# First chunk of a state-space scan: B and C loaded by rows of four tokens and turned once for all batches

## Chip, cores and metric

One NeuronCore of a Trainium2 chip runs the whole kernel. The metric is device time in microseconds, from the first to the last instruction with what lies around them; the median of the runs is quoted.

## What is computed

Inputs: `x` [4 batches, 8 heads, 768 tokens, 32], decays `a` [4, 8, 768], `B` and `C` [4, 8, 768, 16], three weight matrices (256 x 1536 twice, 1536 x 256), all float32. First a scan with decay, in chunks, then a gated feed-forward layer on its 3072 x 256 result:

```python
cum = np.cumsum(np.log(a_chunk), axis=-1)
L = np.exp(cum[..., :, None] - cum[..., None, :]) * causal
M = np.einsum('bhin,bhjn->bhij', Cc, Bc) * L
y = M @ xc + (Cc @ state) * np.exp(cum)[..., None]
state = decay_full * state + sum_j(Bc_j xc_j * decay_from_j)
...
gate = 1 / (1 + np.exp(-(y @ w_gate)))
out = (gate * (y @ w_val)) @ w_out
```

## The kernel before

The 768 tokens are taken in six chunks of 128 (two halves of 64 each). Chunk 0 is worked batch by batch by the class `FirstUnit`, one unit for each of the four batches; later chunks by the class `Scan`, all batches together. Of a unit: `spread` has TensorE multiply `apart` (the clipped decays of all batches, one head's in each column block) by `of_unit`, which copies a batch's decays to all partitions (tile `pa`), and VectorE runs a multiplying scan over it (tile `ab`). `products` turns the batch's B and C (tile `pt`), ScalarE copies them out (`bct`), TensorE forms the products C B (`pcb`). `before` and `decays` make C and B with decays (`cd`, `bd`). `result` weighs `pcb` with the scan (`m`), multiplies by `x` (`py`, `mm`), VectorE keeps the right blocks (`sm`, `mr`), TensorE adds the part of the first half's state, and ScalarE takes the result out (`xw`, in `take`). `state` makes the state that chunk 1 starts from. `first_products` makes the running products of the decays (`pp`).

The feed-forward layer then runs over column tiles f = 0 to 11 of each chunk of 512 rows. For chunk 0, f = 0 is worked in halves (`halves_of`, tile `pgv`), f = 1 to 5 with plain float32 weights (`gate` and `value`, tiles `pg` and `pv`), and from f = 6 on in the format fp32r with high and low parts of the weights (`part_w`, tile `w`) and of x (`parts_of_x`, tiles `xh` and `xl`). `split_w` rounds the weights (tile `wr`): two VectorE steps, two of ScalarE, one of GpSimd. Float32 matmuls of 512 columns leave two records in the trace, fp32r ones a single record.

All loads of the head are issued on SyncE's queue: the decays, then B and C of a batch with two DMAs each (`load_bc`: 128 partitions, for each of 8 heads one piece of 16 numbers, 64 bytes), then x (pieces of 128 bytes) and the weights (pieces of 2 KB). Three PSUM buffers (`ps_mm`) go round among `pa`, `pt`, `pp`, `mm` and the feed-forward products; `ps_y` holds one `py`.

The order of everything is made when the program is built: `run` takes generators of steps, each with an engine, a planned cost and needs, and gives each engine the ready step with the lowest place in the table `DUES`, among those that can start soonest. A letter behind a place (d, p, a) fixes the engine where a step can go to two. `keep_warm` adds matmuls on an identity where the plan has TensorE idle; `WARM` lists the matmuls on zeros at the very start (widths in blocks of 128 columns).

Of the kernel before, what the change touches and what calls it, by code (L numbers as in the profile page):

```python
# [8 lines left out]
F32 = mybir.dt.float32  # L9
# [9 lines left out]
    "": "0 1", "b0": "2", "w0": "3", "b3": "4", "b1": "5", "products0": "6 7 9 13 18", "products0_0": "8 11 28",  # L19
    "spread3": "10 15", "split0": "12 16 19 24 32", "b2": "14", "spread1": "17 23", "spread0": "20 29", "x0": "21",  # L20
    "before0_0": "22p 27", "decays0_3": "25", "x1": "26", "products0_1": "30 34 42", "w1": "31", "spread2": "33 41",
    "x3": "35", "result0_0": "36 46 50 56 63 69", "decays0_0": "37p", "products0_3": "38 44 51", "x2": "39",
    "decays0_1": "40", "w2": "43", "before0_1": "45 47d", "products0_2": "48 55 64", "decays0_2": "49",
    "result0_1": "52 60 66 70 77 82", "early0_0": "53", "before0_3": "54p 57", "w3": "58",
    "result0_3": "59 78 87 91 95 98", "bq1_2": "61", "split1": "62 68 79 85 96", "r": "65", "before0_2": "67p 74p",
    "state0_0": "71", "w5": "72", "result0_2": "73 92 99 100 105 111", "early0_1": "75", "w4": "76",
    "xparts": "80 88d 116 209d", "bq1_0": "81", "half0_0": "83 103 112 117", "state0_1": "84", "w13": "86",
    "w6": "89", "early0_3": "90", "split2": "93 97 102 107 115", "bq1_3": "94", "early0_2": "101", "w7": "104",
    "state0_3": "106", "split3": "108d 119 124 126 139", "bq1_4": "109", "half0_1": "110 118 123 128",
    "state0_2": "113", "w9": "114", "w10": "120", "clip": "121 129 135", "gate0_1": "122 134",  # L30
# [12 lines left out]
    "split12": "241d 244 249 253 265", "value0_8": "247 254", "part10": "248 252", "gate0_9": "251 259",
    "split17": "255 262 274 278 282", "value0_9": "256 264", "part11": "257 260d", "split15": "258d 275 284 289 296",
    "gate0_10": "261 268", "split14": "263d 266 270 272 277", "value0_10": "267 276 280d 322", "w16": "269",
    "early1": "271", "gate0_11": "273 281", "value0_11": "279 291 295d 316d",
    "proj0_0": "283 304 337 345 347 350 376", "part17": "285 292", "bq2_4": "286", "decays1": "287 299 300 305 311d",
    "bq2_0": "288", "bq2_6": "290", "bn2": "293", "bq2_2": "294", "part0": "297 308d",
    "proj0_1": "298 325 352 361 364 430 460", "a2_0": "301", "cq2_4": "302", "bq2_5": "303", "bq2_3": "306",
    "cq2_5": "307", "cq2_1": "309", "cq2_6": "310", "part1": "312 336d", "a2_1": "313",  # L50
    "split16": "314 317 320 323 328", "cq2_2": "315", "scan1": "318 332 335 340", "before1": "319d", "bq2_7": "321",
    "cq2_0": "324", "weigh1": "326 329 333 338 344 353 355 357 359", "bq2_1": "327", "cq2_3": "330", "cq2_7": "331",
    "bn3": "334", "part2": "339 341", "state1": "342 349d", "part3": "343 346d", "part4": "348 351d",
    "part5": "354 356d", "part12": "358 360p", "gate1_0": "362 370", "p2_0": "363", "p2_1": "365",
    "value1_0": "366 374 378a 382", "part13": "367 371d", "p2_3": "368", "p2_2": "369", "x2_": "372",
    "gate1_1": "373 381", "part14": "375 377p", "value1_1": "379 387 397 406d", "turned2": "380 384",
# [81 lines left out]
PE0 = 5.6  # L138
# [1343 lines left out]
```

## Time and profile before

| what | value |
|---|---|
| median of 3 runs | 345.69 us (345.6 to 346.02) |
| the profiled execution | 345.54 us |
| its span, first to last instruction | 343.7 us, so 1.84 us lie around it |
| busy share of the span | TensorE 98%, VectorE 64%, GpSimd 52%, ScalarE 44% |

The span is read as a head, in which chunk 0 is scanned and TensorE has gaps, and a rest, in which it has next to none. A busy TensorE is not one at its peak: filler matmuls and cold ones count as busy.

### The profile page before, as it was taken

To read this page: it belongs to the slowest core of one execution; us is meant where nothing else is said; L and a number is where in the kernel's file an instruction comes from. 1 tells how busy PE (TensorE), PEld (TensorE's weight loads), DVE (VectorE), ACT (ScalarE), POOL (GpSimd) and SP (SyncE) were. 2 spreads that over 40 slices of the span, in tenths; PEclk is the share of its full clock that TensorE was granted. 3 is DMA by queue.
4 is the path that set the end of the run, shared out by engine and by line. 5 is a ranking of instruction groups with operands and counts; after the bars stand their busy time and mean duration, and the time that the engine had idled before them with its cause. 6 is when DMAs were issued, how large, how long until landed. Compare 5 with 4: busy or idle time off the path is not lost.

```text
span 343.7 us, 7948 instructions
## 1 busy us (share of the span) xinstructions
PE 337.9 (98%) x3144; PEld 261.7 (76%) x3144; DVE 220.2 (64%) x377; ACT 150.2 (44%) x277; POOL 180.0 (52%) x181
## 2 busy tenths in 40 slices
PE   8899999999999999999999999999999999999996
PEld 3474587457888888888888888888888888888885
DVE  5889978956879872456666954566064646856221
ACT  4476987124744230136411513361047557645300
POOL 4646265431646434566774545489427885355500
PEclk9999999999999999999999999999999999999999
DMA  6996899871674376476543621108123733220032
GB/s 107 180 352 209 256 272 146 162 132 35 94 159 62 90 109 159 97 139 89 145 100 102 85 76 21 63 3 297 72 36 91 240 89 110 110 61 2 0 58 67
DMA packets 100247, 40.16 MB, mean 117 GB/s; under 512 B 88754, under 2 KB 91826, under 8 KB 99570
## 3 DMA queue, kind: packets, MB, share of 16 engines
q1 hardware_dynamic: 97906, 39.39, 49.3%
q10 hardware_dynamic: 2304, 0.26, 0.5%
q8 instruction: 25, 0.41, 0.5%
q14 instruction: 12, 0.10, 0.1%
HBM read 30.00 MB, written 9.63 MB: 115 GB/s over the span
## 4 chain that ended last, share of the span: by engine, by line
PE 98%; DVE 1%; ACT 0%; issue 0%
PE pg L981 17%; PE pv L981 17%; PE ux L1121 6%; PE acc L1121 6%; PE po L1017 5%; PE po L1013 5%; PE po L1019 5%; PE po L1018 5%; PE acc L1224 5%; PE uz L1121 5%; PE pg L972 2%; PE pv L972 2%; PE po L1251 2%; PE pcb L706 2%; PE pcb L691 2%; PE pcb L647 2%
## 5 line engine op out<-in xcount | busy, mean ns | idle before, releaser
L981 PE MATMUL pg<-xh,w 128*128 128x512 f32 x168 | 59.0, 392 | 0.0
L981 PE MATMUL pv<-xh,w 128*128 128x512 f32 x168 | 58.9, 391 | 0.0
L927 POOL TENSOR_TENSOR h<-g,h 128x512 fp32r<-128x512 f32 x27 | 38.3, 1420 | 24.4 <-ACT h L925 17.2
L921 DVE TENSOR_TENSOR g<-pv,g 128x512 f32<-128x512 f32 x38 | 26.1, 688 | 30.1 <-PE pv L981 29.1
L903 ACT ACTIVATE g<-pg 128x512 f32<-128x512 f32 x47 | 28.0, 596 | 39.4 <-PE pg L981 37.2
L981 PEld LDWEIGHTS pg<-xh,w 128*128 128x128 f32 x168 | 31.5, 188 | 6.7
L981 PEld LDWEIGHTS pv<-xh,w 128*128 128x128 f32 x168 | 31.5, 188 | 6.6
L497 POOL TENSOR_TENSOR wr<-wr 128x512 int32<-128x512 int32 x18 | 20.5, 1143 | 26.8 <-ACT wr L495 13.0
L981 PE MATMUL pg<-xl,w 128*128 128x512 f32 x84 | 32.7, 389 | 0.0
L981 PE MATMUL pv<-xl,w 128*128 128x512 f32 x84 | 32.7, 389 | 0.0
L1017 PE MATMUL po<-h,w 128*128 128x512 f32 x76 | 30.8, 405 | 0.0
L1019 PE MATMUL po<-h,w 128*128 128x512 f32 x76 | 29.6, 390 | 0.0
L1018 PE MATMUL po<-h,w 128*128 128x512 f32 x76 | 29.6, 389 | 0.0
L577 DVE TENSOR_TENSOR_SCAN ab<-ab,delta 128x512 f32<-128x512 f32 x20 | 28.1, 1424 | 0.0
L925 ACT CAST h<-g 128x512 fp32r<-128x512 f32 x26 | 16.0, 619 | 24.2 <-DVE g L921 24.0
L1048 POOL TENSOR_TENSOR c<-c,c 128x512 f32<-128x512 f32 x13 | 17.2, 1326 | 17.9 <-ACT c L1176 9.2
L1048 POOL TENSOR_TENSOR h<-c,h 128x512 fp32r<-128x512 f32 x16 | 21.0, 1323 | 9.4 <-ACT h L1200 9.3
L1048 POOL TENSOR_TENSOR sw<-sw 128x128 f32<-128x128 f32 x36 | 18.9, 535 | 11.2 <-DVE sw L1048 10.2
L1028 DVE STREAM_TRANSPOSE o<-po 128x256 f32<-128x256 f32 x16 | 6.3, 430 | 21.2 <-PE po L1019 19.2
L1200 ACT CAST h<-c 128x512 fp32r<-128x512 f32 x24 | 14.9, 619 | 10.7 <-POOL c L1048 7.1
L981 PEld LDWEIGHTS pv<-xl,w 128*128 128x128 f32 x84 | 15.8, 188 | 3.2
L981 PEld LDWEIGHTS pg<-xl,w 128*128 128x128 f32 x84 | 15.8, 188 | 3.2
(197 smaller groups left out, 733.2 us busy)
## 6 DMA issues: line engine op xcount, KB each, us to landing
w_s<-sp SPq DMA_DIRECT2D x12, 512.0 KB
s<-w_s SPq DMA_DIRECT2D x12, 512.0 KB
ab<-a_z SPq DMA_DIRECT2D x10, 512.0 KB
wr<-in_moe_w_gate_dram SPq DMA_DIRECT2D x6, 512.0 KB
wr<-in_moe_w_val_dram SPq DMA_DIRECT2D x6, 512.0 KB
wr<-in_moe_w_out_dram SPq DMA_DIRECT2D x6, 512.0 KB
xn<-in_x_dram SPq DMA_DIRECT2D x5, 512.0 KB
out_dram<-o SPq DMA_DIRECT2D x144, 16.0 KB
```

Of the source, the lines that this page charges most:

```text
L497: nc.gpsimd.tensor_tensor(out=lw.bitcast(I32), in0=hw.bitcast(I32), in1=lw.bitcast(I32), op=ALU.add)
L577: nc.vector.tensor_tensor_scan(out=t, data0=t, data1=delta.rearrange("p h l -> p (h l)"), initial=0.0, op0=ALU.mult, op1=ALU.add,)
L903: nc.scalar.activation(gs[k, f], pm, AF.Sigmoid)
L921: nc.vector.tensor_tensor(out=g, in0=pm, in1=g, op=ALU.mult)
L927: engines[eng].tensor_tensor(out=hl, in0=g, in1=hh.bitcast(F32), op=ALU.subtract)
L981: nc.tensor.matmul(pm, w[:, part, kt, fs], xx[:, kt], start=(i == 0), stop=(i == 3 * NK - 1))
L1013: nc.tensor.matmul(acc, whole[NF + f // 2][:, f % 2, ms], hs[k, f], start=start, stop=stop)
L1017: nc.tensor.matmul(acc, hi, hh, start=start, stop=False)
L1018: nc.tensor.matmul(acc, hi, hl, start=False, stop=False)
L1019: nc.tensor.matmul(acc, lo, hh, start=False, stop=stop)
L1048: engines[eng].tensor_tensor(out=out, in0=in0, in1=in1, op=op)
L1121: nc.tensor.matmul(out, a[i], b[j], start=start and n == 0, stop=n == 2, skip_group_check=True)
```

## The change

B and C of chunk 0 are loaded like those of later chunks, in pieces of four tokens (256 bytes) for each head, onto 32 partitions a batch: four DMAs each, B's on SyncE's queue and C's on ScalarE's. One copy (`sorted_rows`) puts the four tokens of a row apart, four transposes turn all batches at once, and ScalarE writes B (`bt0`), C for both head groups (`cg0`) and C's second half (`ct0`) with the tokens in order; four more transposes of `bt0` give B by tokens (`bn0`). The decays are loaded twice, onto both halves of the partitions; the upper half keeps what rounding to fp32r leaves, so that `spread` is one fp32r product. `chosen_of` lets ScalarE do a step of VectorE's, some copies may go to GpSimd, two of the starting matmuls on zeros become the whole of `WARM`, and the table `DUES` is new throughout (in it `xparts` step 1 goes from VectorE to GpSimd, and the `state0` steps come later).

```diff
-WARM = (4, 4, 3)
-PE0 = 5.6
+WARM = (4, 4)
+PE0 = 4.7
-FIRST = "b0 x0 b1 x1 b2 x2 w0 b3 x3 w1 w2 w3 r w4 w5 w6 w7 w8 w9"
+FIRST = "bq0 w0 x0 x1 w1 x2 x3 w2 w3 r w4 w5 w6 w7 w8 w9"
...
-    of_unit = hp.tile([P, NB, P], F32, tag="h8", name="of_unit")
+    of_unit = hp.tile([P, NB, P], F32R, tag="h8", name="of_unit")
...
-        for tag, src in (("bn", b4), ("cq", c4)):
-            t = quad_of(tag, 0, H, N, bufs=2 if tag == "bn" else 1)
-            nc.sync.dma_start(t[:, b], src[:L, b * H : (b + 1) * H])
+    def load_first(tag, src, eng):
+        t = got[tag, 0] = ld.tile([P, H, NQ * N], F32, tag=tag, name=f"{tag}0", bufs=1)
+        rows = src[:, :, :L].rearrange("b h (t f) n -> b t h (f n)", f=NQ)
+        for b in range(NB):
+            eng.dma_start(t[32 * b : 32 * b + 32], rows[b])
...
+    def chosen_of(eng, out, local):
+        if eng == "dve":
+            return chosen(out.rearrange("p (o c) -> p o c", o=1), local.rearrange("p (o c) -> p o c", o=1), 1)
+        for g in range(NG):
+            gs = slice(g * D, (g + 1) * D)
+            nc.scalar.mul(out[:, gs], local[:, gs], of_g[:, g : g + 1])
...
-            yield step("pe", 0.45, [("bc", b)], [("tp", b)], banks=1)
-            nc.tensor.transpose(pt[:, :L], bn, eye)
-            nc.tensor.transpose(pt[:, L : 2 * L], cn, eye)
-            nc.scalar.copy(self.bct[:, 0], pt[:, :L])
-            for g in range(NG):
-                nc.scalar.mul(self.bct[:, 2 + g], pt[:, L : 2 * L], of_g[:, g : g + 1])
-            nc.scalar.copy(self.bct[:, 1, L2:], pt[:, L + L2 : 2 * L])
+            yield step("pe", 0.47, [("cg0",), ("bt", 0)], [("cb", 0, b)] + [("cb", 0)] * (b == NB - 1))
...
+            multiply(self.pcb, got["bt0"][:, b], got["cg0"][:, b])
...
+        copies[eng](t, got[tag, 0].rearrange("p h (f n) -> p f h n", f=NQ))
...
+        for f in range(NQ):
+            nc.tensor.transpose(pt[:, f * L : (f + 1) * L], got["sorted", tag][:, f].rearrange("p h n -> p (h n)"), eye)
...
+            nc.scalar.mul(got["cg0"][:, :, g].rearrange("p b (t f) -> p f b t", f=NQ), pt, of_g[:, g : g + 1])
+        nc.scalar.copy(got["ct0"].rearrange("p b (t f) -> p f b t", f=NQ), pt[:, :, :, L2 // NQ :])
+        engines[eng].tensor_tensor(out=got["ct0"], in0=got["ct0"], in1=got["p0"], op=ALU.mult)
+        nc.scalar.copy(got["bt0"].rearrange("p b (t f) -> p f b t", f=NQ), pt)
...
+        for b in range(NB):
+            nc.tensor.transpose(pt[:, b * L : (b + 1) * L], got["bt0"][:, b], eye)
+        nc.scalar.copy(t.rearrange("p b h n -> p (b h n)"), pt)
...
-    nc.gpsimd.memset(apart[R2:], 0.0)
-    nc.sync.dma_start(a0, av[:, :L].rearrange("k (o l) -> o k l", o=2))
+    for r, eng in enumerate((nc.sync, nc.scalar)):
+        eng.dma_start(a0[r * R2 : (r + 1) * R2], av[:, :L].rearrange("k (o l) -> o k l", o=2))
+    load_first("cq", Cm, nc.scalar)
     nc.scalar.activation(table, table, AF.Sigmoid)
...
+    nc.vector.tensor_copy(ah, ac)
+    nc.vector.tensor_tensor(out=ah[R2:], in0=ac[R2:], in1=ah[R2:].bitcast(F32), op=ALU.subtract)
```

## Rows read from the trace of the kernel before

**Rows 1.** The page, busy time and share of the span by engine.
```profile
PE 337.9 (98%) x3144; PEld 261.7 (76%) x3144; DVE 220.2 (64%) x377; ACT 150.2 (44%) x277; POOL 180.0 (52%) x181
```

**Rows 2.** Waits of TensorE, whole span: total us, times, longest.
```profile
PE py L706 <- ACT xw L834: 0.5, 1, 0.5
```

**Rows 3.** Timeline of TensorE: start us, us, engine line op out<-in xcount.
```profile
12.63 0.24 PE L706 MATMUL py<-m,xn 64*32 64x64 f32 x1
...
21.66 2.86 PE L962 MATMUL pgv<-xw,wr 128*128 128x256 f32 x12
...
41.53 0.83 PE L289 MATMUL pg<-eye 128*128 128x128 f32 x6
42.12 0.48 PE L981 MATMUL pg<-xh,w 128*128 128x512 f32 x1
```

**Rows 4.** Timeline of all engines, first 8 us.
```profile
0.74 1.28 ACT L1285 ACT_TABLE_LOAD   x1 [0.74 <-PEq L1465]
0.75 0.70 SPq L1283 DMA_DIRECT2D a<-in_a_dram  x1
...
3.24 0.23 DVE L1287 TENSOR_SCALAR ac<-a 64x64 f32<-64x64 f32 x1 [0.26 <-DMA a<-in_a_dram]
...
3.63 0.68 DVE L1289 TENSOR_TENSOR apart<-ac,head 64x512 f32<-64x512 f32 x1
...
3.82 0.34 PEld L237 LDWEIGHTS warm<-warm_sb 128*128 128x128 f32 x1 [0.52 <-issue]
...
4.67 0.34 PEld L237 LDWEIGHTS warm<-warm_sb 128*128 128x128 f32 x1 [0.52 <-issue]
...
6.19 1.02 PE L741 MATMUL pa<-apart,of_unit 128*128 128x512 f32 x2
...
7.25 1.22 DVE L744 TENSOR_TENSOR_SCAN ab<-pa,delta 128x512 f32<-128x512 f32 x1
```

**Rows 5.** Timeline of VectorE, ScalarE and GpSimd, chunk 0 and the start of f = 6.
```profile
11.38 0.69 DVE L695 TENSOR_TENSOR m<-pcb,ab 128x512 f32<-128x512 f32 x1
...
13.44 0.21 DVE L724 TENSOR_TENSOR sm<-py,mask 128x64 f32<-128x64 f32 x1
...
18.83 1.21 DVE L890 TENSOR_TENSOR xl<-xw,xh 128x512 fp32r<-128x512 f32 x1
...
20.73 0.23 DVE L724 TENSOR_TENSOR sm<-py,mask 128x64 f32<-128x64 f32 x1
...
41.19 0.68 DVE L890 TENSOR_TENSOR xl<-xw,xh 128x512 fp32r<-128x512 f32 x1
...
21.78 0.27 ACT L834 COPY xw<-mm 128x128 f32<-128x128 f32 x1 [0.53 <-PE mm L820]
...
18.46 1.04 POOL L497 TENSOR_TENSOR wr<-wr 128x512 int32<-128x512 int32 x1 [2.62 <-ACT wr L495]
```

**Rows 6.** Stretches: busy us (instructions) by engine, granted clock, DMA share, GB/s.
```profile
3.00:6.00 3.00, 3.00 (x6) 1.25 (x5) 1.25 (x4) 0.00 (x0) 2.01 (x5) 1.00 0.87 190
...
7.00:21.00 14.00, 12.48 (x306) 7.53 (x306) 12.33 (x24) 8.17 (x28) 6.93 (x13) 1.00 0.98 210
...
9.00:10.50 1.50, 1.50 (x21) 0.65 (x20) 1.50 (x2) 0.00 (x0) 1.50 (x3) 1.00 0.90 89
...
12.00:13.50 1.50, 1.28 (x66) 1.03 (x66) 1.50 (x4) 0.75 (x4) 0.63 (x3) 1.00 0.73 184
...
16.00:19.00 3.00, 2.46 (x76) 1.76 (x63) 2.33 (x10) 2.25 (x6) 0.54 (x1) 1.00 0.94 337
```

**Rows 7.** Groups by line and shape, 0 to 22 us: busy us, mean ns | idle before.
```profile
L695 DVE TENSOR_TENSOR m<-pcb,ab 128x512 f32<-128x512 f32 x4 | 2.7, 687 | 0.7 <-PE pcb L691 0.6
L765 ACT ACTIVATE bct<-pt,of_g 128x128 f32<-128x128 f32 x8 | 2.5, 374 | 0.0
...
L691 PE MATMUL pcb<-bct 32*64 32x128 f32 x64 | 1.9, 292 | 0.5 <-DVE m L695 0.5
...
L888 ACT CAST xh<-xw 128x512 fp32r<-128x512 f32 x1 | 0.6, 619 | 0.0
```

More of the change, by code (lines that the diff above doesn't have):

```diff
@@ L509, in part_w @@
             needs.append(("used", order[n - 2]) if order[n - 2] < NF else ("proj", 0))
-        yield step("act", ACT_SB, needs)
+        eng = yield step(("act", "pool"), (ACT_SB, 0.75), needs)
         hw, lw = halves.pop(i)
         hi, lo = parts_of(i)
-        nc.scalar.copy(hi, hw)
+        copies[eng](hi, hw)
         eng = yield step(("dve", "pool"), (DVE_SB, POOL_SB), [], [("w", i)], port=True)
@@ L791, in decays @@
             b = self.b
-            eng = yield step(("dve", "pool"), (0.28, 0.42), [("bc", b), ("scan", 0, b)], [("bdec", 0, b)], port=True)
+            eng = yield step(("dve", "pool"), (0.28, 0.42), [("bn0",), ("scan", 0, b)], [("bdec", 0, b)], port=True)
             if ("bd", 0) not in got:
@@ L825, in result @@
             self.take(1)
-            yield step("dve", 0.21, [], [("after", 0, b)], banks=-1)
+            eng = yield step(("dve", "act"), (0.21, 0.45), [], [("after", 0, b)], banks=-1)
             if ("mr", 0) not in got:
@@ L879, in tile_ssd_then_gated_ffn, with first_bn @@
+    def first_bn():
+        yield step("pe", 0.6, [("bt", 0)], banks=1)
+        pt = ps_mm.tile([P, 512], F32, tag="mm", name="pt_bn")
+        keep_warm(pt)
+        for b in range(NB):
+            nc.tensor.transpose(pt[:, b * L : (b + 1) * L], got["bt0"][:, b], eye)
+        yield step("act", ACT_MM, [], [("bn0",)], banks=-1)
+        t = quad_of("bn", 0, H, N, bufs=2)
+        nc.scalar.copy(t.rearrange("p b h n -> p (b h n)"), pt)
     hs, xb, xw, yw = {}, {}, [], {}
@@ L1062, in weight_sums @@
             sum_up(eng, out, in0, in1, op)
-        yield step("act", ACT_SB)
+        eng = yield step(("act", "pool"), (ACT_SB, 0.7))
         parts = hp.tile([P, 2, 512], F32R, tag="r1", name=f"sp{i}")
-        nc.scalar.copy(parts[:, 0], t[:, 1])
+        copies[eng](parts[:, 0], t[:, 1])
         eng = yield step(("dve", "pool"), (DVE_SB, POOL_SB), port=True)
@@ L1346, in initial @@
     def initial():
[L1348 removed]
+        made = [(k, c) for k in ("bt", "ct", "cd", "bdec") for c in (-1, 0) if c < 0 or k in ("cd", "bdec")]
         made += [("y", -1), ("first", 0, -1)]
```

87 lines of the change are left out of this document (53 added, 34 removed), and 233 rows, old and new, of the table DUES.

## The prediction

> **What bounds the kernel.** I read the page's busy shares first, then TensorE's waits, then its timeline, and only then the other engines, in the stretch where TensorE has gaps. TensorE is busy for 98% of the span [rows 1] and its longest wait on another engine after the start is 0.5 us [rows 2]. In the timeline the reader sees two parts. Up to 21.66 us its work comes in short pieces with gaps (the first unit's result begins at 12.63 us); from 21.66 on, feed-forward products of chunk 0 stand end to end [rows 3]. So the time is that of the moment at which TensorE gets into its unbroken part, plus work that this change leaves alone. A microsecond off the head is one off the total, as long as the engines that feed TensorE later come forward too; the place to watch is f = 6, where at 41.53 us fillers stand for 0.59 us before the first fp32r product at 42.12 [rows 3], which waits for the low part of x, begun by VectorE at 41.19 and 0.68 us long [rows 5].
>
> What sets the 21.66? Between 7 and 21 us VectorE is busy 12.33 of 14 us (88%), ScalarE 8.17 and GpSimd 6.93 [rows 6]. VectorE carries the four scans (1.22 us each [rows 4]), the four weighings (0.69 [rows 7]), the block picks, weight steps and an early `xl` of 1.21 us [rows 5]. Its last pick (`sm` of the last unit) is at 20.73 and the last take at 21.78 [rows 5]. VectorE's list sets the end of the head, and it starts only at 7.25, with the first scan [rows 4].
>
> **The change, step by step.**
>
> *Decays.* They land at about 3.24 us, `apart` is made from 3.63 to 4.31, the cold matmuls run to beyond 5.5 (weight loads at 3.82 and 4.67, 0.85 apart), the first spread runs at 6.19 for 1.02 us, and the scan begins at 7.25 [rows 4]. The change adds to VectorE a copy and a subtraction of 64 columns; the nearest row is the clip, 0.23 us [rows 4], so between 0.2 and 0.46 for both, and I take 0.4: `apart` is ready at 4.7. That it now spans 128 partitions costs nothing by rows: 64 partitions took 0.68 [rows 4], 128 took 0.69 [rows 7]. Two cold records of 384 columns go, each three quarters of 0.85 us, together 1.28, so the cold matmuls end by about 4.7 as well. The spread becomes one fp32r record of 512 columns, 0.48 us [rows 3], instead of 1.02. The first scan can start at 4.7 + 0.48 + 0.05, say 5.25: **2.0 us earlier**. Bounds: 1.4 (decays land 0.6 later, behind more DMAs) to 2.2. The memset of `apart` on GpSimd goes too, off the path.
>
> *B and C.* Eight DMAs of 64-byte pieces become eight of 256-byte ones, 8192 pieces become 2048, the bytes stay at 0.52 MB. While 64-byte pieces dominate, the DMA engines are 90% busy and move 89 GB/s; with x's 128-byte pieces 184; with mostly weights 337 [rows 6]. So B and C took some 5.8 us of the engines and now take between 2.85 (at 184) and 1.55 (at 337). On the queues: after the decays' issue, which ends at 1.45 [rows 4], four issues of at most 0.70 end at 4.25, and a landing follows an issue by 1.8 (1.45 to 3.24). That gives 6.0 us for B, bounds 5.2 and 7.0. ScalarE issues five DMAs itself, and its table load of 1.28 us now comes behind them: 4.25 + 1.28 = 5.5, before C is there. x and the weights, behind B on SyncE's queue, come forward by the 3 to 4 us of DMA time that is saved.
>
> *Turning.* Per batch two transposes and four ScalarE copies go (eight of these copies alone take 2.5 us [rows 7]). From B's landing to the first weighing there are now a copy of 512 columns (0.62, by the cast [rows 7]), four transposes (0.29 each at most, by the 128-column products; they overlap, so 0.7), a copy out (0.62), 16 products (1.9 / 4 = 0.48 [rows 7]) and four handovers of some 0.15: 3.0 us. So the first weighing starts at about 9.0, or 9.8 if the copies queue behind C's (0.62 each) and the three PSUM buffers; before it was at 11.38 [rows 5]. The first unit's result follows 1.25 us later as before (11.38 to 12.63), at 10.3 to 11.1. The turn back for `bn0` (0.7 + 0.62, and then `bd`) lies beside the weighing.
>
> *VectorE's list.* From its first scan to the last `sm` it took 20.73 - 7.25 = 13.5 us. `xl` moves to GpSimd (1.21), two state updates of some 0.2 (size of `sm`) move behind, one small step comes in: 13.5 - 1.3 = 12.2. From 5.25 that ends at **17.4, 3.3 us earlier**. By units: results at 10.8, 0.81 to the first `sm` (12.63 to 13.44), and three more units at a pace between 1.4 (0.81 + a take of 0.27 [rows 5] and handovers) and the old 2.43 ((20.73 - 13.44) / 3): 15.8 to 18.9, with 2.0 in the middle 17.6. Both agree; I take 3.3 for the head, bounds 1.8 to 4.9. The `xl` step beside GpSimd's own work at 18.46 took 1.21 instead of 0.68 [rows 5], so moving it to GpSimd may stretch a neighbour by up to 0.5; this is in the bounds.
>
> *f = 6 and the rest.* GpSimd and ScalarE get choices (copies of weight parts) and the table places the `split13` steps behind the last part of x, two VectorE steps fewer before it. The 0.59 us of fillers can go; I take 0.3, bounds 0 and 0.6. The rest of the new table I cost at nothing, since TensorE has no other wait there to lose; a new gap there is the cost if the cover is gone, bounded by the 0.5 of the largest present wait for each.
>
> **Sum.** 345.54 - 3.3 - 0.3 = 341.94 for a profiled execution; the median stands 0.15 above it: **342.1 us**. With all bounds of one side: 345.69 - 5.5 = 340.2 and 345.69 - 1.8 = 343.9.
>
> **Rivals.**
>
> *The head's gain is given back at f = 6.* TensorE reaches f = 1 earlier, but the weights need VectorE, ScalarE and GpSimd steps, and `xl` was the last by 0.25 us (41.87 against 42.12). If these come forward only by the 2.0 us of the first scan, minus 0.5 of stretched neighbours, the total gains 1.5: 344.2. For it: VectorE's 88% before. Against it: `xl`'s first part and `split13` are taken off.
>
> *TensorE stays cold.* The cold records stand 0.85 us apart, the spread's two records of the same columns took 1.02 together [rows 4]: the first ran at 1.2 GHz, the second at 2.4, though the stretch from 3 to 6 us reads a granted clock of 1.00 [rows 6]. What came before the rise was some 4.5 us of unbroken matmuls. Now 3.4 us of them are followed by short pieces. If the unit results ran at 1.2 GHz, each unit would cost up to 0.81 more, four 3.2, and the products and transposes some 1.2: 4.4 us, and 346.5 in all; if only half of the head does, 344.3. The fillers of `keep_warm` speak against it. The Trainium skill ("TensorE: Matmul & The Clock Gate", Part 1) says that the throttled clock is the default and sustained activity releases it; the rise between 5.5 and 6.2 us agrees, and by it a thinner head could stay slow.
>
> *Slower: B and C land late.* Nothing of chunk 0 can be weighed until all four batches of both have landed and been turned, where before one batch was enough. The point at which this decides is a landing of B at 11.38 - 3.0 = 8.4 us: each microsecond beyond is one lost. At the rate of the 64-byte pieces (0.52 MB at 89 GB/s, from 2.7 us) it would be 8.5 plus the landing; with w0's 0.5 MB in between, 10: 347.3. Against it: the rate doubled from 64 to 128 bytes. The Trainium skill ("DMA: Bandwidth & Descriptors", Rules for kernel authors) says that spreading DMAs over issuing engines brings no bandwidth, only issue time, since all run on the same 16 engines; the 90% busy engines agree. By it the second queue saves nothing here, and the landing is that of both together.
>
> *Hidden anyway.* If weights, not scan, bounded the 21.66, nothing would change: 345.7. Against it: the weights' DMAs are not waited for there, and they come earlier too.
>
> **Chances.** Forecast (gain of 2.2 to 5.5 us) 0.66; given back at f = 6 0.13; a larger gain, up to 6.3 us, 0.04; cold for half of the head 0.05, for all of it 0.02; late landing 0.05; hidden or a new gap of the same size 0.05. Measurement tells about 0.2% (0.7 us) from no change. Faster: 0.66 + 0.13 + 0.04 + 0.03 = 0.86; same 0.06; slower 0.08. The likeliest case's own range is 340.2 to 343.5; with the given-back and half-cold cases 339.8 to 344.9.
>
> **What would show it.** Right: first scan near 5.3 us, first weighing near 9 to 10, last `sm` near 17.5, the unbroken part of TensorE from near 18.3, and f = 6 without fillers near 38.3; DMA engines at 180 GB/s or more before 6 us. Wrong: a first weighing beyond 11, matmuls of the units twice as long, fillers or waits of microseconds between f = 2 and f = 8, or new waits of TensorE beyond 60 us.

## The result, and the profile after

| what | before | after |
|---|---|---|
| median of 7 runs | 345.69 us (345.33 to 346.02) | 347.84 us (347.39 to 350.32) |
| ratio | | 1.0073, 95% interval 1.0049 to 1.0097 |
| the profiled execution, its span | 345.54, 343.7 us | 350.32, 348.5 us |

The change makes the kernel 2.15 us slower. Forecast were 342.1 us, 339.8 at least and 344.9 at most. The profiled execution after is the longest of its seven, so its 4.8 us of added span are more than the median's loss; the text says where a part is known to be its own.

The page says what it said before [rows 1]: TensorE is as busy as ever.

```profile
PE 339.9 (98%) x3166; PEld 264.5 (76%) x3166; DVE 228.0 (65%) x391; ACT 150.8 (43%) x267; POOL 170.4 (49%) x168
```

The view of TensorE's waits shows something new beside [rows 2]: 2.3 us in one piece, ended by no engine.

```profile
PE pg L1018 <- issue: 2.3, 1, 2.3
...
PE pg L1027 <- DVE g L967: 0.5, 1, 0.5
```

The timeline of the head answers to [rows 3 to 5].

```profile
4.06 0.25 DVE L1334 TENSOR_SCALAR ac<-a 128x64 f32<-128x64 f32 x1 [1.08 <-DMA a<-in_a_dram]
...
6.24 3.45 DVE L750 TENSOR_TENSOR_SCAN ab<-pa,delta 128x512 f32<-128x512 f32 x3 [0.28 <-PE pa L747]
...
6.99 0.61 POOL L874 COPY rows_cq<-cq 128x512 f32<-128x512 f32 x1 [2.54 <-DMA cq<-in_C_dram]
7.65 0.66 PE L881 MATMUL pt_cq<-eye,rows_cq 128*128 128x128 f32 x4
...
8.34 2.16 ACT L894 ACTIVATE cg<-pt_cq,of_g 128x512 f32<-128x512 f32 x2 [3.04 <-PE pt_cq L881]
...
10.28 1.13 ACT L912 COPY bt<-pt_bq 128x512 f32<-128x512 f32 x1
...
11.46 0.48 PE L689 MATMUL pcb<-cg,bt 32*64 32x128 f32 x16 [0.50 <-ACT bt L912]
...
12.05 0.69 DVE L693 TENSOR_TENSOR m<-pcb,ab 128x512 f32<-128x512 f32 x1 [0.91 <-PE pcb L689]
...
13.01 0.60 ACT L923 COPY bn<-pt_bn 128x512 f32<-128x512 f32 x1
```

The first scan came 1.0 us earlier than before, the first weighing 0.67 later. VectorE has three of its four scans done at 9.7 us, takes two weight steps and waits for the products; the fourth scan follows the first weighing, at 12.65. The first gate product of f = 1 starts at 24.95, where it was 24.36 (first view before, second after), so the head lost 0.59 us.

```profile
18.53 1.14 PE L962 MATMUL pgv<-xw,wr 128*128 128x256 f32 x4
...
24.36 1.88 PE L972 MATMUL pg<-xw,wr 128*128 128x512 f32 x4
```

```profile
20.79 1.03 PE L1008 MATMUL pgv<-xw,wr 128*128 128x256 f32 x4
...
24.95 1.88 PE L1018 MATMUL pg<-xw,wr 128*128 128x512 f32 x4
```

The last `sm` is 0.17 us earlier than before (20.56 for 20.73), and yet f = 1 is later. In between stand the first four products of f = 0: before, TensorE did them at 18.53, in a gap of the head; after, they come behind the last unit's results, at 20.79, and fillers stand in the gap (18.79, 0.71 us long). What holds them there no run tested.

The timeline around f = 4, TensorE, then VectorE, then the queue of SyncE:

```profile
33.75 1.88 PE L1018 MATMUL pv<-xw,wr 128*128 128x512 f32 x4
37.92 2.96 PE L1018 MATMUL pg<-xw,wr 128*128 128x512 f32 x4 [2.29 <-issue]
...
32.69 1.74 DVE L1357 TENSOR_TENSOR_SCAN a<-a,az 32x768 f32<-32x768 f32 x1
36.27 0.43 DVE L480 TENSOR_SCALAR wr<-wr 128x512 f32<-128x512 f32 x1 [1.83 <-DMA wr<-in_moe_w_gate_dram]
...
37.14 0.68 DVE L963 TENSOR_TENSOR h<-pv,g 128x512 f32<-128x512 f32 x1
...
15.61 3.77 SPq L442 DMA_DIRECT2D bq<-in_B_dram  x5
...
23.61 3.22 SPq L442 DMA_DIRECT2D cq<-in_C_dram  x4
```

VectorE stands 1.83 us before a clamp whose weight has not landed. Behind the clamp waits `h` of f = 2, which empties a PSUM buffer; it ends at 37.82 and TensorE goes on at 37.92. On SyncE's queue chunk 1's row loads (`load` of `bq`, `cq`, 32 KB each) stand between the weights. After the wait the granted clock is lower, and two groups of matmuls take 2.75 and 2.47 us from start to start where the others take 1.72, so they lose 1.03 and 0.75:

```profile
38.00:42.00 4.00, 4.00 (x6) 1.75 (x7) 3.97 (x5) 2.72 (x5) 2.48 (x2) 0.59 1.09 227
```

The slow clock is this execution's own: its mean granted clock is 0.995, that of the other six 0.999 to 1.000. From f = 1 to the start of f = 6 it is 21.22 us, before 17.76. The wait adds 2.45 (33.75 to 37.92, less the usual 1.72), the two slow groups 1.78, two short delays at f = 3 some 0.2; the 0.59 of fillers are gone, and the first product of f = 6 starts 1.32 after the last group instead of 1.72, 0.40 less. From f = 6 to the end of the span it is 302.33, before 301.58. So 0.59 + 3.46 + 0.75 = 4.8. Of the 0.75 some 0.3 come of the mark: without fillers ahead of it the first product of f = 6 starts 0.63 us before the second (46.17 and 46.80), with them 0.31 (42.12 and 42.43). The 0.5 that TensorE waits for `g` of f = 5, at 107 us, are the rest.

### The profile page after: what moved, and what is told of

It reads as the page before. It is cut to its first block, busy times and chain, and to the rows that moved or that the text cites. A ratio compares the mean times of both kernels' runs of the same rounds, so it can differ in the third digit from the quotient of the medians.

```text
span 348.5 us, 7993 instructions
## 1 busy us (share of the span) xinstructions
PE 339.9 (98%) x3166; PEld 264.5 (76%) x3166; DVE 228.0 (65%) x391; ACT 150.8 (43%) x267; POOL 170.4 (49%) x168
## 4 chain that ended last, share of the span: by engine, by line
PE 89%; DVE 2%; DMA 2%; issue 1%; SPq 1%; DVEq 0%
PE pg L1027 14%; PE pv L1027 14%; PE ux L1167 6%; PE acc L1167 5%; PE po L1063 5%; PE po L1059 5%; PE po L1064 5%; PE po L1065 5%; PE acc L1270 5%; PE uz L1167 5%; PE pg L1018 3%; PE pv L1018 3%; PE po L1297 2%; PE pcb L704 2%; PE pcb L689 2%; PE pcb L645 2%
## 5 line engine op out<-in xcount | busy, mean ns | idle before, releaser
L973 POOL TENSOR_TENSOR h<-g,h 128x512 fp32r<-128x512 f32 x20 | 28.6, 1431 | 29.0 <-ACT h L971 27.8
L495 POOL TENSOR_TENSOR wr<-wr 128x512 int32<-128x512 int32 x18 | 21.3, 1186 | 33.5 <-ACT wr L493 33.3
L971 ACT CAST h<-g 128x512 fp32r<-128x512 f32 x34 | 21.0, 619 | 32.9 <-DVE g L967 32.6
L1094 POOL TENSOR_TENSOR c<-c,c 128x512 f32<-128x512 f32 x14 | 19.8, 1418 | 19.5 <-PE uz L1167 12.6
L575 DVE TENSOR_TENSOR_SCAN ab<-ab,delta 128x512 f32<-128x512 f32 x20 | 29.1, 1475 | 0.0
L1094 POOL TENSOR_TENSOR sw<-sw 128x128 f32<-128x128 f32 x27 | 15.2, 565 | 18.3 <-DVE sw L1094 17.4
L1270 PE MATMUL acc<-h,w 128*128 128x512 f32 x72 | 18.3, 390 | 0.0
```

The costliest lines, as they stand in the source:

```text
L495: nc.gpsimd.tensor_tensor(out=lw.bitcast(I32), in0=hw.bitcast(I32), in1=lw.bitcast(I32), op=ALU.add)
L575: nc.vector.tensor_tensor_scan(out=t, data0=t, data1=delta.rearrange("p h l -> p (h l)"), initial=0.0, op0=ALU.mult, op1=ALU.add,)
L973: engines[eng].tensor_tensor(out=hl, in0=g, in1=hh.bitcast(F32), op=ALU.subtract)
L1094: engines[eng].tensor_tensor(out=out, in0=in0, in1=in1, op=op)
L1270: nc.tensor.matmul(got["acc"][m], a, b, start=(j == 0 and n == 0 and q == 0), stop=(q == 2), skip_group_check=True)
```

## Experiments

All are compared with the kernel before, run on the same chip (medians 345.55 to 345.77). The table reads each profiled execution, one of 4 to 12, by the same marks, from TensorE's timeline; before, spread_only, spread_twice and rows_early have fillers ahead of f = 6, which sets that mark 0.3 us later there.

| kernel | median (lowest to highest), us | profiled | f = 1 starts | f = 6 starts | f = 6 to end of span |
|---|---|---|---|---|---|
| before | 345.69 (345.33 to 346.02) | 345.54 | 24.36 | 42.12 | 301.6 |
| after | 347.84 (347.39 to 350.32) | 350.32 | 24.95 | 46.17 | 302.3 |
| contig | 347.21 (346.55 to 347.45) | 346.55 | 24.05 | 42.56 | 302.1 |
| one_queue | 347.71 (346.39 to 348.1) | 346.39 | 25.04 | 41.95 | 302.7 |
| spread_only | 348.16 (345.73 to 349.3) | 347.49 | 26.57 | 44.33 | 301.4 |
| spread_twice | 345.51 (345.13 to 346.25) | 346.25 | 25.02 | 42.77 | 301.6 |
| clamp_late | 347.66 (347.5 to 348.11) | 347.66 | 24.98 | 43.20 | 302.7 |
| h_first | 347.33 (345.58 to 348.96) | 345.58 | 24.48 | 41.37 | 302.4 |
| two_edits | 347.05 (345.6 to 348.23) | 348.23 | 26.86 | 43.63 | 302.8 |
| rows_early | 347.63 (347.01 to 347.68) | 347.63 | 24.18 | 43.49 | 302.3 |
| rows_late | 352.11 (350.81 to 353.12) | 352.41 | 29.86 | 46.86 | 303.7 |
| warm_only | 348.23 (347.23 to 348.46) | 347.23 | 25.36 | 43.19 | 302.2 |
| warm_two | 347.3 (345.79 to 347.8) | 347.71 | 24.45 | 41.98 | 303.9 |
| warm_best | 345.95 (345.06 to 346.7) | 346.7 | 24.95 | 42.33 | 302.6 |
| rows_mid | 349.49 (348.25 to 351.02) | 349.14 | 26.87 | 43.86 | 303.4 |
| mid_best | 347.71 (347.3 to 347.96) | 347.56 | 27.42 | 44.18 | 301.6 |
| more_instr | 350.33 (349.41 to 351.25) | 350.39 | 27.92 | 44.69 | 303.9 |
| first_weights | 349.5 (347.7 to 351.38) | 350.0 | 27.99 | 44.88 | 303.3 |
| later_weights | 345.54 (344.43 to 347.7) | 344.51 | 24.50 | 41.27 | 301.4 |
| wide_fill | 348.27 (346.94 to 350.17) | 346.94 | 24.25 | 41.66 | 303.2 |

### The head: the turned copies and the second queue

**contig.** The three copies of `cg`, `ct` and `bt`, for instance:

```diff
-        nc.scalar.copy(got["bt0"].rearrange("p b (t f) -> p f b t", f=NQ), pt)
+        nc.scalar.copy(got["bt0"].rearrange("p b (t f) -> p b t f", f=NQ), pt.rearrange("p f b t -> p b t f"))
```

> The changed kernel with the order inside ScalarE's copies of the turned B and C turned round: they write in order and read PSUM with steps, instead of reading in order and writing every fourth number. Theory A (the writes with steps are what makes a copy of 512 columns take 1.08 to 1.13 us instead of 0.60): each copy falls to about 0.6 to 0.7, bt0 is ready 1.4 us earlier (at 10.0), the first result starts near 12.9 instead of 14.13; the wait at f = 4 stays, and the total falls by 0 to 1.4 us, 346.5 to 347.8. Theory B (reading with steps costs as much, or another work beside it is the cause): copies stay at 1.0 us or more and the median within 0.4 us of 347.84.

Ratio 1.0045 (1.0032 to 1.0057), 0.63 us less than after: theory A held, and it is a part of the loss. Timeline of contig:

```profile
8.26 1.27 ACT L894 ACTIVATE cg<-pt_cq,of_g 128x512 f32<-128x512 f32 x2 [2.93 <-PE pt_cq L881]
9.41 0.59 ACT L912 COPY bt<-pt_bq 128x512 f32<-128x512 f32 x1
9.88 0.40 ACT L897 COPY ct<-pt_cq 128x256 f32<-128x256 f32 x1
...
11.14 0.69 DVE L693 TENSOR_TENSOR m<-pcb,ab 128x512 f32<-128x512 f32 x1 [0.46 <-PE pcb L689]
```

The same bytes take 1.27 + 0.59 + 0.40 = 2.26 us instead of 2.16 + 1.13 + 0.68 = 3.97, and the first weighing and f = 1 both come 0.9 us earlier. Steps on the writing side cost nearly the double (1.13 for 0.59), steps of 128 columns on the reading side in PSUM nothing (0.59, and 0.60 for the copy `bn` of after, which does both in order). The Trainium skill ("SBUF — State Buffer", Door 1) says that SBUF has lines of 16 bytes and that each access that crosses to a new line pays a penalty, whose size it does not give; a write with a step of four float32 is on a new line each time, and the trace agrees.

**one_queue.**

```diff
-    load_first("cq", Cm, nc.scalar)
+    load_first("cq", Cm, nc.sync)
```

> The changed kernel with C's four loads on SyncE's queue, ahead of B's four, and none on ScalarE's. If issue time counts (the second queue has a use): C lands near the same time as before, 6.5 to 7.0, B some 2 us later than the 6 to 7 us of now, near 8.5, and the first weighing moves from 12.05 to 13 or later; the time is 348.3 to 349.5. If the engines of the transfers bound it, both landings move by less than 0.5 us and the time stays at 347.4 to 348.2.

1.0055 (1.0040 to 1.0071): like after. The copy of C, which waits for its landing, began 1.47 us earlier and nothing followed:

```profile
5.52 0.61 POOL L874 COPY rows_cq<-cq 128x512 f32<-128x512 f32 x1 [1.18 <-DMA cq<-in_C_dram]
7.34 0.62 POOL L874 COPY rows_bq<-bq 128x512 f32<-128x512 f32 x1 [0.30 <-POOL apb L853]
7.68 0.63 PE L881 MATMUL pt_cq<-eye,rows_cq 128*128 128x128 f32 x4 [0.22 <-DVE ab L750]
8.34 2.15 ACT L894 ACTIVATE cg<-pt_cq,of_g 128x512 f32<-128x512 f32 x2 [4.94 <-PE pt_cq L881]
...
12.03 0.69 DVE L693 TENSOR_TENSOR m<-pcb,ab 128x512 f32<-128x512 f32 x1
```

The transposes of C wait for the first scan, which reads one of the three PSUM buffers until some 7.5 us; so C's landing (its copy begins at 6.99 in after) was not what bounded the chain, the buffers and ScalarE were. Neither line of the expectation came out whole: the landings moved, the time did not. In this profile there is no wait before f = 4 either (f = 6 starts at 41.95), though the order around it is the changed kernel's. The Trainium skill ("DMA: Bandwidth & Descriptors", Rules for kernel authors) says that further issuing engines bring no bandwidth, only issue time. The trace agrees as to the issue time: the eight issues end at 4.27 us with two queues and at some 5.6 with one. No run here shows the bandwidth by itself.

### The spread alone, and TensorE's clock

**spread_only** is the kernel before with the decays loaded twice and the spread as one fp32r product, the old table and starting matmuls.

```diff
-    apart = hp.tile([P, H, L2], F32, tag="h2", name="apart")
+    apart = hp.tile([P, H, L2], F32R, tag="h2", name="apart")
```

> The kernel before with the decays' part of the change alone: decays loaded twice on two queues, rounded product and rest, the spread as one fp32r product; loads of B and C, starting matmuls and the table of places as before. If the earlier scan is worth what the prediction says, the first scan starts near 6.5 instead of 7.25 (the cold matmuls still end near 5.9) and the median falls by 0.3 to 0.8 us, to 344.9 to 345.4. Rival: the two more VectorE steps and the later landing of the decays (4.0 instead of 3.2 in the changed kernel) eat it, and the median stays within 0.3 us of 345.69.

1.0065 (1.0041 to 1.0088), slower, which neither theory had foreseen. Two lines of its timeline, and its stretches (columns as in [rows 6]):

```profile
7.32 0.43 DVE L480 TENSOR_SCALAR wr<-wr 128x512 f32<-128x512 f32 x1 [1.65 <-DMA wr<-in_moe_w_gate_dram]
7.66 1.22 DVE L742 TENSOR_TENSOR_SCAN ab<-pa,delta 128x512 f32<-128x512 f32 x1
```

```profile
8.00:10.00 2.00, 1.07 (x19) 0.62 (x19) 2.00 (x3) 1.29 (x3) 1.16 (x3) 1.00 1.04 98
10.00:12.00 2.00, 1.20 (x5) 0.48 (x3) 1.90 (x3) 0.90 (x4) 1.80 (x4) 0.72 1.01 142
12.00:14.00 2.00, 1.80 (x66) 1.15 (x65) 1.68 (x3) 0.90 (x4) 1.14 (x4) 0.50 0.90 236
```

The spread was done at 6.31, but the scan stood behind a clamp that waited for its weight, so the shorter spread gained nothing. And TensorE, with less to do (1.07 us of 2 from 8 to 10 us, where it was 2.00 before), fell to 1.2 GHz (granted clock 0.50) until some 21 us. All seven executions show it: their mean granted clock is 0.980 to 0.989.

**spread_twice** issues the same product twice, nothing else.

```diff
+            for _ in range(2): nc.tensor.matmul(pa, of_unit[:, b], ...)
```

> The kernel before with the spread alone as one fp32r product, and this product issued twice, which gives TensorE back the busy time of the old one and nothing else. Theory (the spread alone lost time because TensorE's clock fell between 10.7 and 20.5 us): the granted clock stays at 1.00 in the head and the time is 344.8 to 345.9 us. Rival (the double load of the decays and the steps of VectorE cost the time): 347 to 348.5 as with the single product, and the clock makes no difference.

0.9995 (0.9987 to 1.0004): the clock stays at 1.00 (stretches of spread_twice; all eleven executions have 0.998 to 1.000) and the loss is gone, though the double load, VectorE's two added steps and the clamp ahead of the scan (at 7.38) are still there. "TensorE stays cold" was a true mechanism of the cheaper spread. In the changed kernel the granted clock is 1.00 from 4 to 22 us; that its fillers do this was not tested.

```profile
10.00:12.00 2.00, 1.62 (x18) 0.70 (x6) 1.90 (x3) 0.89 (x4) 1.80 (x4) 1.00 0.98 137
12.00:14.00 2.00, 1.55 (x74) 1.16 (x82) 1.88 (x4) 0.98 (x5) 1.13 (x4) 1.00 0.73 185
```

### The wait before f = 4

**clamp_late** sets the clamp of w8 behind `h` of f = 2; **h_first** sets that `h` ahead of the long scan of the decays as well; **two_edits** is h_first with contig. (In the last two, nine steps of `split_w` are also fixed to VectorE.)

```diff
+DUES.update({"split8": "172 173 195 201 213"})                               # clamp_late
+DUES.update({"split8": "173d 175 195 201 213", "value0_2": "157 161", ...})  # h_first
-        yield step("dve", 1.8, [("z",)], [("p",)], port=True)
+        yield step("dve", 1.8, [("z",), ("h", 0, 2)], [("p",)], port=True)
```

> The changed kernel with one step of VectorE moved: the clamp of weight w8 comes behind the product h of f = 2 instead of ahead of it. Theory 1 (VectorE waits 1.83 us at 36.27 for w8's load, the h steps queued behind it keep a PSUM buffer, and TensorE stands for 2.29 us from 35.63): the wait of TensorE goes or falls below 0.8 us, the granted clock stays at 1.0, and the median falls from 347.84 to about 345.5 to 346.3. Theory 2 (VectorE simply has too much to do around f = 4): the wait moves to the next h and the median stays within 0.7 us of 347.84.

> The changed kernel with one order changed on VectorE: the step h of f=2 stands ahead of the long scan of all decays and of the clamp that waits for a late weight. Theory 1 (the 2.3 us that TensorE waits before f=4 are a wait for the PSUM buffer which that h gives back): the wait is 0.5 us or less, and the time is 345.5 to 346.5 us. Rival (TensorE waits there for the weights of f=4, which are loaded too late, and h only happens to end at the same moment): the wait stays at 1.2 us or more and the time at 347.4 to 347.9.

> The same order, and ScalarE's copies of the turned B and C write in order and read with steps. If the two causes are separate, their gains add: 0.6 us from the copies and what the other order gives alone, so 344.9 to 345.9 us, and the first feed-forward product of f=1 near 24.05 us. Rival (they share one wait, that of the weights): no more than the better of the two alone, 346.5 to 347.3.

In all profiles with the wait TensorE goes on 0.10 us after that `h` ends (after 37.82 and 37.92, clamp_late 36.55 and 36.65, contig 35.91 and 36.01), and with `h` first the wait is 0 and f = 6 starts at 41.37. So theory 1 of h_first, a wait for the buffer, holds for the wait. That it makes the median does not follow:

```profile
36.65 1.96 PE L1019 MATMUL pg<-xw,wr 128*128 128x512 f32 x4 [1.21 <-issue]
```

In clamp_late the clamp is behind `h` and the wait is still 1.21 us (the line above), not below 0.8: `h` still stands behind the long scan. The medians are 1.0062, 1.0050 and 1.0034, all three above what theory 1 or "the gains add" had; the profile of h_first is the fastest of eight, which scatter from 345.58 to 348.96, and without any edit to that order one_queue shows no wait. The wait's length thus changes between executions, and the 2.3 us of the longest one are not the loss of the median.

**rows_early** is the kernel before with nothing but chunk 1's row loads ahead of the weights of f = 2 and later.

```diff
+DUES.update({"bq1_0": "61", ..., "bq1_7": "61", "cq1_0": "88", ..., "cq1_7": "88"})
```

> The kernel before with nothing but the row loads of chunk 1 (16 loads of 32 KB) moved ahead of the weights of f=2 and later on SyncE's queue, as the changed kernel has them. Theory (those early loads delay the weights, and VectorE's steps behind them): slower by 0.7 to 3 us, with a wait of TensorE between f=1 and f=6. Rival (the loads fit in, since the DMA engines are busy 0.6 of the time between 28 and 36 us): 345.3 to 346.0 us.

1.0052 (1.0040 to 1.0064), 1.9 us lost, as the theory had it. Stretches of before and after, 14 to 22 us, and of rows_early, 18 to 26 us, where its row loads stand; the last two columns are the share of the DMA engines and GB/s:

```profile
14.00:18.00 4.00, 3.05 (x110) 2.14 (x99) 3.70 (x10) 2.73 (x10) 1.61 (x4) 1.00 1.01 246
18.00:22.00 4.00, 3.88 (x108) 3.04 (x108) 3.11 (x9) 1.97 (x7) 1.04 (x1) 1.00 1.05 331
```

```profile
14.00:18.00 4.00, 3.65 (x124) 2.91 (x123) 4.00 (x8) 2.10 (x8) 3.74 (x7) 1.00 0.78 172
18.00:22.00 4.00, 4.00 (x126) 3.20 (x124) 2.52 (x10) 3.33 (x8) 1.90 (x2) 1.00 0.45 109
```

```profile
18.00:22.00 4.00, 4.00 (x112) 3.18 (x90) 3.28 (x9) 2.18 (x7) 1.04 (x1) 1.00 0.53 169
22.00:26.00 4.00, 4.00 (x16) 2.85 (x16) 3.13 (x11) 2.29 (x5) 2.07 (x4) 1.00 0.71 184
```

Timeline of rows_early, SyncE's queue, then TensorE:

```profile
16.42 5.77 SPq L445 DMA_DIRECT2D bq<-in_B_dram  x8
24.32 7.56 SPq L445 DMA_DIRECT2D cq<-in_C_dram  x8
41.34 2.39 PE L290 MATMUL pg<-eye 128*128 128x128 f32 x20
```

Sixteen row loads of 32 KB hold SyncE's queue for 5.77 + 7.56 us, 0.83 each on average: 0.53 to 0.57 for the median one, up to 2.1 for single ones. A weight of 512 KB takes 0.47 (median). So half a megabyte in rows holds the queue as long as many weights do; the DMA engines are less busy (0.53 where it was 1.05) and the weights come late. The loss shows as 2.39 us of fillers before f = 6, twenty records where [rows 3] has six.

### The scatter: not the start of TensorE

**warm_only** puts the third block of starting matmuls back, **warm_two** adds it to two_edits, **warm_best** also sets VectorE's step on C of chunk 2 behind `g` of f = 5.

```diff
-WARM = (4, 4)
+WARM = (4, 4, 3)
+DUES.update({"before2": "430d"})  # warm_best alone
```

> The changed kernel with the third block of starting matmuls on zeros put back (384 columns, 0.6 us of cold work ahead of the first spread, which waits for the decays there anyway). Theory 2 (the shorter start makes the rise of TensorE's clock come late in some executions, and a late rise costs the head up to 2.4 us): the spreads take 0.97 us for three in the profiled execution, the span of the times shrinks below 1 us, and the median falls to 346.3 to 347.3. Rival (times scatter for another reason, the transfers): median and scatter as in the changed kernel, 347.4 to 348.5.

> The copies in order and h of f=2 first, as before, and the third block of starting matmuls as well. Theory 2: the scatter of 2.6 us (345.6 to 348.2 without the block) shrinks below 1 us and the median comes to the fastest of those, 345.0 to 345.8. Rival: 346.3 to 347.3 with the old scatter.

> As the one with order, copies and starting block, and VectorE's step on C of chunk 2 stands behind g of f=5, for which TensorE waits 0.5 us near 103 us. If that wait is TensorE's own time, 0.3 to 0.6 us less than the kernel without this last edit; if the wait moves on, the same within 0.2 us.

Theory 2 fell: 1.0073, 1.0047 and 1.0009, and warm_two's times still run over 2 us. It came from two_edits, whose profiled execution had slow spreads (1.65 us for three, 0.97 in contig); that costs single executions, it does not make the scatter. The last edit takes the wait of 0.5 us for `g` away, and the median fell by 1.35 where 0.3 to 0.6 were expected, more than this wait explains.

### The order of loads, and standstills of TensorE

**rows_late** sets all row loads behind the weights; **rows_mid** sets two between each two weights, **mid_best** adds the other edits to it.

```diff
+DUES.update({"bq1_0": "140", ..., "cq1_0": "149", ..., "turned1": "190 240"})              # rows_late
+DUES.update({"w3": "50", "bq1_2": "52", "bq1_5": "53", "w4": "54", "bq1_6": "55", ...})    # rows_mid
```

> The changed kernel with chunk 1's sixteen row loads of B and C placed behind the weights w4 to w9 and w11 on SyncE's queue (and chunk 1's turning steps later on VectorE). Theory 1 (the small row loads ahead of the weights make w4 to w8 land late): w8 lands before 30 us, TensorE has no wait at f = 4, the head is unchanged, and the median is 344.8 to 346.0. Theory 2 (VectorE overloaded): TensorE still waits 1 us or more near f = 4 or f = 6, and the median stays at 347 or above.

> The changed kernel with another order of loads on SyncE's queue alone (and chunk 1's turning on VectorE after it): x and the weights of f=0 to 3 first, then two of chunk 1's row loads between each two weights, where the changed kernel issues nine of these sixteen before the fourth weight. Theory 3 (the early row loads hold up the weights: between 14 and 22 us the transfers fall to 172 and 109 GB/s where they were 246 and 331, and the wait before f=4 and its scatter come of that): 250 GB/s or more between 14 and 22 us, no wait before f=4 beyond 0.5 us, 345.3 to 346.5 us, all times within 1 us. Rival (the order of VectorE's steps alone makes the wait): the transfers rise, the wait and its scatter stay, 347 to 348.

> The same loads with all the other edits that helped: ScalarE's copies in order, h of f=2 early, VectorE's step on C of chunk 2 behind g of f=5. If the causes add: 1.0 to 1.5 us below the row order alone, 344.0 to 345.2 us, faster than the kernel before. Rival (the gains share one wait): the same as the row order alone within 0.4 us.

With the weights ahead of the row loads or between them the wait before f = 4 is gone in all three, as theory 3 wants (16.8 to 17.0 us from f = 1 to f = 6, before 17.76). But the ratios are 1.0188, 1.0117 and 1.0059, far above what was expected of all three: something new stands in the head, which loses 2.5 to 5.5 us there (start of f = 1). Timeline of mid_best:

```profile
16.10 0.38 PE L286 MATMUL mm<-eye 128*128 128x128 f32 x1
18.73 0.49 PE L286 MATMUL mm<-eye 128*128 128x128 f32 x3 [2.26 <-issue]
```

These are fillers. They read a constant, and the view names nothing that ended the idle time between the first and the second. **more_instr** is mid_best with more instructions and no more work at the start:

```diff
-WARM = (4, 4)
+WARM = (1, 1, 1, 1, 1, 1, 1, 1)
```

> The last kernel (all edits, weights and row loads in turns), whose TensorE stands still for 2.3 us between two filler matmuls that read only a constant, after 221 of its matmuls and 222 weight loads. Here the starting matmuls have the same columns in 8 pieces instead of 2, which is 12 matmul and 12 weight-load records more and no more work. Theory 4 (TensorE has come to the end of the instructions that it holds, and the next packet of them comes late behind the weights): the stall stands again after 221 or 222 of each, which is now 12 matmuls earlier in the program, among the products of unit 1. Rival (something at that place of the program holds it, a buffer or a semaphore that the profile does not name): it stays at the same filler, after 233 and 234.

1.0132 (1.0111 to 1.0154). Timeline of more_instr, then the stretch from 0 to within the standstill of mid_best and of more_instr; in brackets the records of TensorE, matmuls and weight loads:

```profile
15.68 0.22 PE L714 MATMUL mm<-xn,bd 64*32 64x64 f32 x1
17.91 0.21 PE L714 MATMUL py<-xn,bd 64*32 64x64 f32 x1 [2.02 <-issue]
```

```profile
0.00:17.50 17.50, 14.97 (x221) 10.43 (x222) 13.69 (x30) 7.74 (x18) 9.17 (x21) 1.00 0.86 201
```

```profile
0.00:17.50 17.50, 14.23 (x221) 11.99 (x222) 13.24 (x28) 7.35 (x17) 9.15 (x21) 1.00 0.86 204
```

The place in the program moved, the count of 221 and 222 stayed, as theory 4 had it (rows_mid has it too). A second standstill comes at 347 and 347, 251 records on: 2.6 us in rows_late, 0.4 in two_edits, 0.65 in more_instr (there 347 and 348). The page lists instructions as transfers of their own, in two queues; this is the larger:

```profile
q8 instruction: 25, 0.41, 0.5%
```

(page of mid_best) If these are TensorE's, 25 packets for 3166 + 3166 records are 253 each, which fits the 251. Read by stretches of 0.25 us, TensorE goes on 2.2 to 2.7 us after such a packet begins (mid_best 16.0 and 18.73, more_instr 15.5 and 17.91, rows_mid 16.5 and 18.98, rows_late 22.5 and 25.09). In after the packets begin at 14.0 and 19.0, and TensorE comes to these counts at 17.0 and 21.6: no standstill. That points to TensorE running out of instructions, whose packet begins too late. That the weights hold it up is an inference: in mid_best and rows_mid the DMA engines carry some 308 GB/s between 14 and 16 us, in after 127.

**first_weights** keeps the order of the changed kernel up to the fourth weight and sets two more weights ahead of five row loads, with all the other edits.

```diff
+DUES.update({"w4": "51", "w5": "52", "w6": "86", "w7": "104", "w8": "106", ...})
```

Expected were, if theory 4 holds, a standstill of 0.5 to 2 us in the head and 345.5 to 347.5 us; if only the weights matter (theory 3), none, and 344.2 to 345.3. The ratio is 1.0107 (1.0081 to 1.0134): slower than both. Its timeline, and the stretch from 0 to within the standstill:

```profile
23.49 0.69 PE L809 MATMUL mm<-cd,sm 128*64 128x64 f32 x7 [2.04 <-issue]
```

```profile
0.00:23.30 23.30, 19.54 (x347) 14.12 (x347) 15.81 (x38) 11.05 (x26) 11.63 (x23) 1.00 0.78 199
```

The standstill is there, 2.04 us, and at the second count. From 14 to 16 us the DMA engines carry 127 GB/s and there is none at 221; from 18 to 20 they carry 371, the next packet begins at 20.75 instead of 19.0, and TensorE stands at 347. So theory 4's standstill came where it was expected; the time it had too small.

**later_weights** keeps the order of the changed kernel to 21 us, sets the next three weights ahead of seven row loads, and has all the other edits. **wide_fill** writes up to four fillers as one instruction.

```diff
+DUES.update({"w6": "90", "w7": "91", "w8": "98", "cq1_2": "104", "turned1": "119 172", ...})  # later_weights
+            nc.tensor.matmul(to[:, : r * P]..., eye, eye...broadcast_to([P, r, P]), ...)       # wide_fill
```

> Loads in the order of the changed kernel up to 21 us, then the three next weights ahead of seven row loads instead of between them; the other edits the same. Transfers are light while the head's instruction packets are wanted (to 20 us), so no stall in the head by theory 4; the weights of f=6 and later come 2 to 5 us earlier than in the changed kernel, so by theory 3 no wait before f=6: 344.3 to 345.4 us and times within 1.2 us. If the scatter has another cause: 345.5 to 346.7 as with the copies, order and start block, whose median was 345.95.

> The last kernel (next weights after 21 us), with the filler matmuls of up to four blocks of 128 columns written as one instruction of up to 512 columns: the same columns, some 15 matmuls fewer up to 20 us. Theory 4 (the scatter of 344.4 to 347.7 us comes of instruction packets that are late in some executions): TensorE needs the second packet later, so fewer executions stall, the scatter shrinks below 2 us and the median comes to 344.4 to 345.2 us. Rival (the scatter has another cause, or the packets are asked for later too): median 345.3 to 345.9 and a scatter of 3 us as before.

later_weights: 1.0000 (0.9980 to 1.0021), as fast as before, so these edits together give back the whole loss; its best execution, 344.43, is below all of before (the profiled one, 344.51, has neither wait nor standstill). But the median is just above the expected range, and the times run over 3.3 us, from 344.4 to 347.7, where 1.2 were expected. wide_fill, 1.0089 (1.0059 to 1.0119), did not lessen the scatter and lies above both of its ranges: theory 4 does not explain the scatter. What makes single executions differ by 3 us, and why wide_fill is 2.7 us slower than later_weights, stays open.

## Why the prediction was wrong

| step | predicted | measured |
|---|---|---|
| first scan | 5.25 | 6.24 |
| landing of B and C | 6.0 | C just before 6.99, of no effect |
| first weighing | 9.0 to 9.8 | 12.05 |
| pace of the units | 2.0 | 1.89 (first results at 14.13, last 19.81) |
| last `sm` | 17.4 | 20.56 |
| fillers at f = 6 | 0.3 to 0.6 gained | gone, 0.59 |
| rest of the table | 0 | in this profile the wait of 2.3 before f = 4 and 0.5 for `g` of f = 5 |

*Decays.* The double load landed 0.8 us later (4.06 for 3.24), where the bound allowed 0.6, and the scan came 1.0 us earlier, outside the bounds of 1.4 to 2.2. From the landing to the scan it took 2.18 us, 2.0 by the prediction: that part was right.

*B and C: the first step that failed.* The chain of 3.0 us had one copy out of 0.62 us, and the upper value of 9.8 added 0.8 for C's copies and the three PSUM buffers. On ScalarE stand two for C (2.16) and one for B (1.13) ahead of the products, 3.3 us; contig shows that 1.4 us of these come of writing with a step, for which the prediction had no term. And its start was taken from the landing, while the transposes could not begin before the PSUM buffer was free at 7.6 (one_queue). 7.65 for the transposes, 0.69 to the copies, 3.1 to the end of `bt`, 0.6 to the weighing is the 12.05.

*VectorE's list.* Its length from the first weighing on was as forecast: the last `sm` 8.5 us later, 20.56 (predicted 8.4 from 9.0). That the list starts with the scan, and that the scan's microsecond is therefore the head's, was wrong: the list waits for the products until 12.05. Nor does its last pick alone set the end of the head: from the last `sm` to f = 1 it took 3.63 us before and 4.39 after, because the first products of f = 0 no longer lie in a gap. Of the 3.9 us by which the head missed its forecast (3.3 gained forecast, 0.6 lost), 3.1 are the late first weighing and 0.8 this.

*"The rest of the new table I cost at nothing": the second step that failed.* It makes the smaller part of the miss (some 1.9 of 5.8 us by the estimate below) and the larger part of the loss against before. The cover was named, the queue was not gone through: the sixteen row loads of chunk 1, set ahead of the weights, cost 1.9 us even in the old kernel (rows_early). The bound of 0.5 for a new gap was the longest wait under the old order, which bounds nothing under a new one. Three of the prediction's own signs of being wrong came: a first weighing beyond 11 us, a wait of microseconds between f = 2 and f = 8, and a new wait beyond 60 us (0.5 at 107).

*The rivals.* "B and C land late" had the right sign and the wrong mechanism: they landed in time. "TensorE stays cold" is true of the spread alone (spread_only, spread_twice). "Given back at f = 6" had no gain to give back, since the head itself lost; f = 6 lost its fillers, and the loss behind the head lies before f = 4 and at `g` of f = 5. Its reason, engines that feed TensorE and do not come forward, was near: the weights come late.

*The size.* Of the prediction's sum the lower gain was 1.8, in its chances 2.2; the measured loss is beyond either. How the 2.15 us of the median divide is not shown, since each profile is one execution of a kernel whose times scatter. An estimate from clamp_late, whose profile is at its own median of 347.66: of its 2.2 us of added span some 0.6 lie before f = 1, some 0.8 from there to f = 6 and some 0.8 behind it (the mark of f = 6 set right by 0.3), 0.5 of the last in the wait for `g`. The 1.9 of rows_early cannot be added to the 0.6 of the head: they are the whole loss of another kernel, from f = 1 to the end. That weights come late, ScalarE's stepped copies and the place of VectorE's step on C of chunk 2 are each a part is shown by rows_early, contig and the waits; that there is no further part is not.

## What to carry to other kernels

Go through each queue load by load when an order changes: here a small load held the issuing queue no shorter than one of sixteen times the bytes, and what landed late showed up far behind, at an in-order engine that waited for it ahead of something unrelated. Before a faster producer is counted as a gain, look for what its consumer waits for next, here a PSUM buffer and a copy engine. Where ScalarE must change the order of elements on the way out of PSUM, as here, let it read with steps and write in order. Before a wait in one profile is called the loss, look whether the profiled execution is a typical one.

## What the runs showed of the hardware

- The page lists 25 transfers of instructions, 0.41 MB; if they are TensorE's, as their number fits, they hold some 253 records each. In a head of many small matmuls, with 300 to 390 GB/s of other transfers ahead of such a packet (mid_best, rows_mid, rows_late, first_weights), TensorE stood still for 1.3 to 2.6 us at the same counts of records wherever these fell in the program, and in mid_best the clock fell behind it (granted 0.50 between 20 and 22 us). That the packet is what it waits for is inferred from counts and times.
- ScalarE's copy of 128x512 out of PSUM: 0.59 us written in order, 1.13 with a step of four float32.
- A row load of 32 KB held SyncE's queue for 0.53 to 0.57 us (median; 0.83 on average in rows_early), a weight of 512 KB for 0.47 (median).
- A cheaper product can cost time: with half the work in its spreads TensorE ran at 1.2 GHz for some ten microseconds and the kernel took 348.16 us; with the same product issued twice the clock stayed up and it took 345.51.
